# Attention scores issued two key tiles at a time, in a kernel whose plan gets new matmul times

## The chip, the core and the metric

The kernel runs on one core of a Trainium2 chip. The metric is device time in microseconds (us), the median of several executions. The kernel before took 481.65 us (480.47 to 483.04) when the prediction was made.

The engines are named as the profile names them: PE is TensorE (matmuls), PEld its weight loads, DVE is VectorE, ACT is ScalarE, POOL is GpSimd, SP is SyncE, which here only issues DMAs.

## The reference, cut to what matters

```python
batch, n_heads, seq, head_dim = (8, 12, 448, 64)
q_n, k_n = rmsnorm(q, g_q), rmsnorm(k, g_k)          # over head_dim
attn = softmax(matmul(q_n, k_n.T) / sqrt(64))
x = matmul(attn, v)                                  # -> (3584 tokens, 768)
h = x @ w_in                                         # 768 -> 2048
g = h * clip(h + 3, 0, 6) / 6
out = g @ w_out                                      # 2048 -> 768
```

The kernel works on 48 head pairs (8 batches of 6 pairs). One head has only 64 rows to contract, so the scores of the two heads of a pair use the upper and the lower half of the matmul array at once (in the trace of the kernel before, the two matmuls start 0.003 to 0.004 us apart). All other matmuls contract 112 or 128 rows.

## The kernel before

The kernel is not emitted in the order in which it is written. Every piece of work is recorded as a step with an engine, an estimated duration, a due time and its dependencies. A small list scheduler then replays these on modelled engines and emits the steps in the order of their modelled start. This fixes the instruction order of every engine when the program is built. The durations are only a model: on the chip nothing but the order is left of them.

```python
def order(self):                      # of class Plan, cut
    while len(done) < len(self.steps):
        # the engine that can start something first, by the model
        s = min((s for s in open_[e] if ready[id(s)] <= at), key=lambda s: (s.due, s.n))
        s.start = at
        free[e] = at + s.dur
        ...
    return sorted(done, key=lambda s: (s.start, s.n))
```

A step whose inputs are not ready in the model is passed over for one that is, whatever their due times.

PSUM holds two score buffers S, one buffer X and one R for the value products, and two buffers M shared by the MLP's matmuls. Per pair, four key tiles of 112 columns are scored and exponentiated:

```python
START, FIRST, SECOND, SLOT = 9.0, 4.1, 5.4, 7.9     # modelled length of a pair: 1st batch, 2nd, later
S_r = Ring(tiles("S", 2, [128, 2, 512], FP32, psum))
...
for t in range(T):                                   # T = 4
    ps, swar, s_use = S_r.take()
    def score(t=t, ps=ps):
        for a in range(2):
            rows = slice(a * 64, a * 64 + 64)
            nc.tensor.matmul(out=ps[:, a, 0:S], lhsT=kp[rows, t * PT:t * PT + 128],
                             rhs=kq[rows, 1, :], start=True, stop=True)
    s = add("PE", 0.25, at + step * t / T, score, *ks, *swar)
    x = add("ACT", 0.85, at + step * t / T + 0.2, ...EXP..., s, *war)
```

The work that feeds a pair ("preparation") runs on other engines: POOL squares q and k (sq), DVE sums (ssq), ACT makes rs, POOL scales (qks), SP issues a DMA transpose (kq<-qks), DVE makes kp.

## Time and profile before

| | before |
|---|---|
| time, median | 481.65 us |
| PE busy of 48 us, 160 to 208 and 208 to 256 us | 47.92 and 48.00 |
| first scores of pairs 3, 10 and 15 | 35.6, 95.0 and 130.9 us |
| twelve pairs, 24 to 36 | 103.4 us |

The first fence is from the page's groups; the columns after the first bar are busy time in all (us) and the mean of one (ns), then idle time of the engine just before them, with what ended most of it.

```profile
L336 PE MATMUL S<-kq,kp 64*128 64x448 bf16 x384 | 71.2, 384 | 11.1 <-ACT e L340 6.4
L336 PEld LDWEIGHTS <-kp 64*128 64x128 bf16 x384 | 18.2, 94 | 51.7 <-issue 41.9
```

The weight loads of the scores come after 41.9 us in which the weight loader waits for nothing that the profile shows. The next one is the table of stretches of the kernel before (start and end in us, length, then busy time of each engine):

```profile
core 0: us, PE busy (x) PEld busy (x) DVE busy (x) ACT busy (x) POOL busy (x), PEclk, DMA share, GB/s
64.00:112.00 48.00, 40.56 (x399) 22.02 (x395) 31.62 (x53) 33.89 (x60) 38.76 (x34) 0.96 0.76 159
112.00:160.00 48.00, 44.64 (x363) 22.32 (x364) 35.07 (x51) 30.22 (x57) 41.61 (x35) 1.00 0.86 197
208.00:256.00 48.00, 48.00 (x408) 24.41 (x407) 26.19 (x47) 29.09 (x47) 22.61 (x20) 1.00 0.62 148
```

From about 120 us PE is the bound; earlier it is not. A piece of PE's timeline (start, length, what) shows what a score costs:

```profile
208.79 0.36 PE L336 MATMUL S<-kq,kp 64*128 64x448 bf16 x2
209.08 0.43 PE L351 MATMUL X<-va,e 112*128 112x65 bf16 x8
209.45 0.36 PE L336 MATMUL S<-kq,kp 64*128 64x448 bf16 x2
209.74 0.43 PE L351 MATMUL X<-va,e 112*128 112x65 bf16 x8
210.01 0.42 PE L351 MATMUL R<-va,e 112*128 112x65 bf16 x8
```

Lengths overlap, so read the starts. Eight value matmuls take 210.01 - 209.74 = 0.27 us before more of their kind, but 209.45 - 209.08 = 0.37 before scores. The two matmuls of a lone key tile keep the array from 209.45 to 209.74, 0.29 us.

### The profile page before, as it was taken

The numbers are of one execution on the slowest core, as the hardware profiler recorded it, in microseconds if no ns is written. First come the engines' busy times: TensorE is split into PE (matmuls) and PEld (weight loads), VectorE is DVE, ScalarE is ACT, GpSimd is POOL, SyncE is SP. The second block draws the span as 40 slices with busy tenths as digits, with TensorE's granted clock in tenths as the row PEclk, the third lists the DMA queues.
The fourth block names the chain that finished last, engine by engine and source line by source line (L and its number), as shares of the span: only waits on it lengthen the run. The fifth ranks groups of instructions, "written<-read, shape, count | busy, mean of one in ns | idle before, by whom it ended". The sixth has DMA issues, their size and how long they took to land.

```text
span 480.8 us, 9258 instructions
## 1 busy us (share of the span) xinstructions
PE 436.2 (91%) x3658; PEld 237.9 (49%) x3658; DVE 246.6 (51%) x429; ACT 253.3 (53%) x421; POOL 220.9 (46%) x218
## 2 busy tenths in 40 slices
PE   0667698968999999999999999999999999999996
PEld 0334454534444555555445565554545555644463
DVE  2636457565877775454566445544444343433421
ACT  3445454885567565656676466655655555322200
POOL 7834866998789853655354634652231000000000
PEclk9985699998999999999999999999999999999999
DMA  7999984999787845766458567562413312211122
GB/s 190 245 245 240 251 183 111 187 194 210 194 231 135 204 102 132 169 169 160 117 132 154 134 148 174 120 172 55 99 29 73 78 49 51 59 34 33 34 64 67
DMA packets 103531, 65.26 MB, mean 136 GB/s; under 512 B 62400, under 2 KB 100032, under 8 KB 103488
## 3 DMA queue, kind: packets, MB, share of 16 engines
q1 hardware_dynamic: 98048, 58.38, 51.5%
q0 software_dynamic: 5440, 6.29, 7.4%
q8 instruction: 28, 0.46, 0.4%
q14 instruction: 15, 0.12, 0.1%
HBM read 45.61 MB, written 11.01 MB: 118 GB/s over the span
## 4 chain that ended last, share of the span: by engine, by line
PE 71%; POOL 10%; issue 8%; DMA 6%; DVE 2%; ACT 2%; POOLq 0%; ACTq 0%
PE M L472 30%; PE M L447 25%; PE S L336 8%; PE X L351 6%; POOL qks L280 4%; DMA w_in_sb<-in_moe_w_in_dram 4%; POOL sq L259 3%; PE R L351 2%; DMA kq<-qks 2%; POOL va L288 1%; DVE gT L455 1%; ACT t L453 1%; ACT e L340 1%; DVE kp L314 1%; POOL sq L251 0%
## 5 line engine op out<-in xcount | busy, mean ns | idle before, releaser
L340 ACT ACTIVATE e<-S 112x896 bf16<-112x896 f32 x192 | 171.4, 915 | 100.6 <-PE S L336 99.3
L447 PE MATMUL M<-xT,w_in_sb 128*128 128x384 bf16 (+1 forms) x768 | 170.5, 354 | 4.4 <-DVE y L480 1.9
L472 PE MATMUL M<-w_out_sb,gT 128*128 128x384 bf16 x896 | 161.6, 326 | 0.7 <-DVE gT L455 0.3
L280 POOL TENSOR_TENSOR qks<-qk,rs 112x512 bf16<-112x512 f32 x94 | 97.6, 1057 | 94.1 <-DMA kq<-qks 60.2
L455 DVE SCALAR_TENSOR_TENSOR gT<-t,M 128x384 bf16<-128x384 f32 (+1 forms) x128 | 79.2, 619 | 82.6 <-ACT t L453 82.3
L453 ACT ACTIVATE t<-M 128x384 f32<-128x384 f32 (+1 forms) x128 | 69.5, 543 | 81.8 <-PE M L447 78.6
L472 PEld LDWEIGHTS <-gT 128*128 128x128 bf16 x896 | 81.3, 98 | 60.1 <-issue 12.6
L447 PEld LDWEIGHTS <-w_in_sb 128*128 128x128 bf16 x768 | 66.8, 97 | 70.0 <-issue 21.1
L259 POOL TENSOR_TENSOR sq<-qk 112x1024 f32<-112x1024 f32 x41 | 78.5, 1919 | 20.1 <-DMA qk<-in_q_dram 13.8
L351 PEld LDWEIGHTS <-e 112*128 112x128 bf16 x1536 | 71.3, 102 | 31.0 <-issue 10.5
L336 PE MATMUL S<-kq,kp 64*128 64x448 bf16 x384 | 71.2, 384 | 11.1 <-ACT e L340 6.4
L480 DVE COPY y<-M 128x384 f32<-128x384 f32 x56 | 31.2, 557 | 70.0 <-PE M L472 70.0
L351 PE MATMUL X<-va,e 112*128 112x65 bf16 x1152 | 61.9, 201 | 1.9 <-ACT e L340 1.5
L262 DVE TENSOR_REDUCE ssq<-sq 112x16 f32<-112x1024 f32 x48 | 58.0, 1212 | 10.5 <-POOL sq L259 10.3
L288 POOL CAST va<-vf 112x512 bf16<-112x512 f32 x48 | 30.2, 630 | 31.7 <-PE R L351 18.1
L336 PEld LDWEIGHTS <-kp 64*128 64x128 bf16 x384 | 18.2, 94 | 51.7 <-issue 41.9
L314 DVE TENSOR_SCALAR kp<-kq,gp 128x448 bf16<-128x448 bf16 x41 | 24.5, 598 | 13.5 <-PE S L336 9.9
L377 DVE TENSOR_TENSOR xn<-X,rd 128x384 bf16<-128x384 f32 x48 | 26.8, 558 | 1.6
L300 PE MATMUL M<-ident,qks 112*128 112x112 bf16 x56 | 6.9, 284 | 21.5 <-DVE qks L280 14.7
L376 DVE RECIPROCAL rd<-X 128x6 f32<-128x6 f32 x48 | 9.3, 194 | 29.1 <-PE X L351 29.0
L351 PE MATMUL R<-va,e 112*128 112x65 bf16 x384 | 21.7, 201 | 0.0
L269 ACT ACTIVATE rs<-ssq 112x16 f32<-112x16 f32 x48 | 10.4, 216 | 12.7 <-POOL qks L280 6.7
(27 smaller groups left out, 69.3 us busy)
## 6 DMA issues: line engine op xcount, KB each, us to landing
qk<-in_k_dram SPq DMA_DIRECT2D x48, 224.0 KB, 3.6
qk<-in_q_dram SPq DMA_DIRECT2D x48, 224.0 KB, 3.9
vf<-in_v_dram SPq DMA_DIRECT2D x48, 224.0 KB, 3.8
w_in_sb<-in_moe_w_in_dram POOLq DMA_DIRECT2D x4, 768.0 KB, 22.1
w_out_sb<-in_moe_w_out_dram POOLq DMA_DIRECT2D x8, 384.0 KB, 28.5
out_dram<-y SPq DMA_DIRECT2D x8, 336.0 KB, 3.2
out_dram<-y SPq DMA_DIRECT2D x8, 288.0 KB, 2.7
out_dram<-y SPq DMA_DIRECT2D x8, 240.0 KB, 2.8
```

Source lines behind the costliest of these rows:

```text
L259: parts.append(add("POOL", 1.95, at - 12, lambda: nc.gpsimd.tensor_tensor(out=sq[0:PT], in0=qk[0:PT], in1=qk[0:PT], op=MULT), *ld, *war))
L262: red = add("DVE", 1.2, at - 8, lambda: nc.vector.tensor_reduce(out=ssq[0:PT], in_=sq[0:PT].rearrange("p i h (t d) -> p (i h t) d", d=D), ...
L280: nc.vector if e == "DVE" else nc.gpsimd).tensor_tensor(
L288: vc = add("POOL", 0.7, at - 3, lambda: nc.gpsimd.tensor_copy(out=va[0:PT, :, :, 0:D], in_=vf[0:PT].rearrange("p h (t d) -> p h t d", d=D) ...
L336: nc.tensor.matmul(out=ps[:, a, 0:S], lhsT=kp[rows, t * PT:t * PT + 128], rhs=kq[rows, 1, :], start=True, stop=True)
L340: x = add("ACT", 0.85, at + step * t / T + 0.2, lambda t=t, ps=ps: nc.scalar.activation(out=e[0:PT, t], in_=ps[0:PT, :, 0:S], func=EXP), s ...
L351: nc.tensor.matmul(out=dst[:, a * E1:(a + 1) * E1], lhsT=e[0:PT, t, a, c0:c0 + 128], rhs=va[0:PT, a, t, :], start=(first and a == 0 and t ...
L447: nc.tensor.matmul(out=m[:, 0:n], lhsT=w_in_sb[:, kt, f * 128:(f + 1) * 128], rhs=X[:, kt, :], start=(kt == 0), stop=(kt == NKT - 1))
L453: r = add("ACT", 0.08 + n / 1200, due + span, lambda: nc.scalar.activation(out=t[:, 0:n], in_=m[:, 0:n], func=RELU, bias=0.5, scale=1.0 / ...
L455: g = add("DVE", 0.12 + n / 960, due + span, lambda: nc.vector.scalar_tensor_tensor(out=G[:, f, :], in0=t[:, 0:n], scalar=1.0, in1=m[:, 0: ...
L472: nc.tensor.matmul(out=m[:, 0:HALF], lhsT=G[:, f, i * 128:(i + 1) * 128], rhs=w_out_sb[:, f, cols], start=(f == 0), stop=(f == NFT - 1))
L480: c = add("DVE", 0.55, due + span, lambda: nc.vector.tensor_copy(out=y[:, cols], in_=m[:, 0:HALF]), *parts, *(ywar if n == 0 else []))
```

## The change

From the second batch on, two key tiles are scored in one step, so that the array is switched to half-rows and back half as often. Such a cluster takes both score buffers, so it waits until both have been exponentiated. In the same edit the model's times for scores, exps and value products, and the slot of a pair, are set to what the trace shows.

```diff
-    START, FIRST, SECOND, SLOT = 9.0, 4.1, 5.4, 7.9
+    START, FIRST, SECOND, SLOT = 9.0, 4.1, 5.4, 8.3
 ...
-        for t in range(T):
-            ps, swar, s_use = S_r.take()
-            def score(t=t, ps=ps):
-                ... two matmuls, heads a = 0, 1 ...
-            s = add("PE", 0.25, at + step * t / T, score, *ks, *swar)
-            x = add("ACT", 0.85, ...)
+        size = 1 if P < NJ else 2
+        for t0 in range(0, T, size):
+            taken = [S_r.take() for _ in range(size)]
+            def score(t0=t0, taken=taken):
+                for i, (ps, _, _) in enumerate(taken):
+                    ... two matmuls, heads a = 0, 1 ...
+            s = add("PE", 0.2 + 0.196 * size, at + step * t0 / T, score, *ks, *(d for x in taken for d in x[1]))
+            for i, (ps, _, s_use) in enumerate(taken):
+                x = add("ACT", 0.93, ...)
 ...
-            av.append(add("PE", 0.31, ...values...        # also for `rest`
+            av.append(add("PE", 0.27, ...values...
 ...
-    mlp(B - 1, B - 2, end, end + 36.0, 2)                 # also in the line after it
+    mlp(B - 1, B - 2, end, end + 36.5, 2)
```

More of the change, by code (lines that the diff above doesn't have):

```diff
@@ L329, in attend @@
         exps = []
-        for t in range(T):
-            ps, swar, s_use = S_r.take()
-            def score(t=t, ps=ps):
-                for a in range(2):
-                    rows = slice(a * 64, a * 64 + 64)
-                    nc.tensor.matmul(out=ps[:, a, 0:S], lhsT=kp[rows, t * PT:t * PT + 128],
-                                     rhs=kq[rows, 1, :], start=True, stop=True)
-            s = add("PE", 0.25, at + step * t / T, score, *ks, *swar)
-            x = add("ACT", 0.85, at + step * t / T + 0.2, lambda t=t, ps=ps: nc.scalar.activation(
-                out=e[0:PT, t], in_=ps[0:PT, :, 0:S], func=EXP), s, *war)
-            s_use.append(x)
-            exps.append(x)
+        size = 1 if P < NJ else 2
[3 more added lines that the diff above has]
+                for i, (ps, _, _) in enumerate(taken):
+                    for a in range(2):
+                        rows, c0 = slice(a * 64, a * 64 + 64), (t0 + i) * PT
+                        nc.tensor.matmul(out=ps[:, a, 0:S], lhsT=kp[rows, c0:c0 + 128],
+                                         rhs=kq[rows, 1, :], start=True, stop=True)
+            s = add("PE", 0.2 + 0.196 * size, at + step * t0 / T, score, *ks, *(d for x in taken for d in x[1]))
+            for i, (ps, _, s_use) in enumerate(taken):
+                x = add("ACT", 0.93, at + step * (t0 + i) / T + 0.2, lambda t=t0 + i, ps=ps: nc.scalar.activation(
+                    out=e[0:PT, t], in_=ps[0:PT, :, 0:S], func=EXP), s, *war)
+                s_use.append(x)
+                exps.append(x)
             kq_use.append(s)
@@ L357, in attend @@
         for s in range(NS):
-            av.append(add("PE", 0.31, at + 0.15 * step * s, lambda s=s: values(
+            av.append(add("PE", 0.27, at + 0.15 * step * s, lambda s=s: values(
                 X[:, s * 130:(s + 1) * 130], s * 128, s == 0), *exps, vc, *war))
@@ L364, in attend @@
         i = P % 3
-        rest = add("PE", 0.31, at + 0.45 * step, lambda: values(
+        rest = add("PE", 0.27, at + 0.45 * step, lambda: values(
             Rt[:, i * 130:(i + 1) * 130], S - 128, i == 0), *exps, vc, *war)
@@ L549 @@
     end = begin[NP]
-    mlp(B - 1, B - 2, end, end + 36.0, 2)
-    mlp(None, B - 1, end + 36.0, end + 57.0, 0)
+    mlp(B - 1, B - 2, end, end + 36.5, 2)
+    mlp(None, B - 1, end + 36.5, end + 57.0, 0)
     with tc.manual_schedule():
```

## The prediction

> **What bounds the kernel now.** TensorE. In the table of stretches it is busy 47.9 to 48.0 of 48 us in each stretch from 160 to 400 us; ScalarE has 27 to 29 there, VectorE 19 to 28, GpSimd under 28. The chain of waits gives PE 71% of the span. Before about 120 us it is otherwise: PE idles until the first scores (16.5 us), then is starved behind loads, GpSimd (10.0 of 10 us in 80 to 90) and transposes. So from about 120 us on a microsecond of PE work removed is a microsecond of time; before that, nearly nothing.
>
> **What a score costs.** From starts of matmuls in PE's timeline: the two matmuls of one key tile (64 rows each) start 3 ns apart, and the next matmul of another kind 0.295 us after the first. Scores start 0.094 us later than the kind before them would start its next (eight value matmuls take 0.356 us before scores, 0.262 otherwise). Two key tiles in a row take 0.485 us, the second only 0.19. So two lone tiles cost 0.78 us, a cluster of two 0.58: 0.20 us saved. The Trainium skill, "TensorEngine Tiling (Array Packing)", Key Properties, says that changing the tiling mode drains the engine; the trace agrees, with these two gaps.
>
> **What changes in the order.** Comparing the built orders: as many matmuls, loads and activations as before. From the third batch on there are 126 runs of scores before (111 of one tile, 13 of two, 2 of three), 72 after, all of two; in the second batch 16 against 12. 58 fewer at 0.20 us: 11.5 us of PE time; my sum over those spacings goes from 413.4 to 401.9 us. Up to head pair 14 (115 us now) the sums are nearly equal, so it falls where PE is the bound. A pair's slot there goes from 8.6 to 8.3 us, which the new SLOT also says. The tail after the last scores (66 us) stays.
>
> **What it costs.** A cluster needs both score buffers, so it waits for two exps (1.72 us), and ScalarE idles some 0.4 us (scores, hops) before the next. From pair 14 on at least 2.6 us of PE work, mostly over 3.2, stand between clusters, so this should stay hidden. In the burst of pairs 8 to 13 (85 to 110 us), where ScalarE is 85 to 94% busy, only 0.4 to 0.9 us stand between them: PE will wait for exps there, up to 0.4 us a cluster; GpSimd's 4.6 us per pair covers most. I allow 1 us, and 2 us either way for other reordering of the static queues before 125 us (waits of 1.3 and 2.1 us there now).
>
> **Predicted:** 481.65 - 11.5 + 1 = 471.1 us, range 467.5 to 476. Faster by over 2% (under 472.0): 0.58; within 2%: 0.40; slower: 0.02.
>
> **What would show it.** PE's scores in clusters of four matmuls; PEld's idle before scores from 42 us to about 25; twelve pairs in 99.5 us instead of 103.4; PE full from 130 us on; the first score of pair 14 within 2 us of 115.
>
> **What would make it wrong.** A front end that moves by over 3 us; PE waits for exps inside the full stretch; relu evictions behind two exps in a row, so that both M buffers are held; the saved PE time exposing GpSimd (41.6 of 48 us in 112 to 160).

## More of the kernel before

After a pair, DVE normalizes X into xn, and SP transposes it (xT<-xn); the last 64 rows of three pairs go together as xr (xT<-xr). The MLP of a batch can start only when all its xT are there. POOL also issues the loads of the weights:

```python
for c in range(8):
    W_out[c] = add("POOL", 0.9, 36 + 3.5 * c, lambda c=c: load_w_out(c), xfer=2.7)
```

## The result, and the profile after

The changed kernel took 489.91 us (488.99 to 490.32, four runs), the kernel before 482.16 (four runs, three of them those above). The ratio is 1.0162 (95% interval 1.0129 to 1.0195): 1.6% slower, where 2.2% faster was predicted. A ratio here is the mean time of one kernel's runs over that of the other's of the same rounds, so not quite the ratio of the medians quoted.

What the change was meant to do, it did. The same two groups on the changed kernel's own lines:

```profile
L338 PE MATMUL S<-kq,kp 64*128 64x448 bf16 x384 | 61.6, 391 | 6.8 <-ACT e L343 5.7
L338 PEld LDWEIGHTS <-kp 64*128 64x128 bf16 x384 | 12.9, 96 | 26.1 <-issue 21.0
```

PE's timeline shows a cluster in the full stretch:

```profile
221.33 0.55 PE L338 MATMUL S<-kq,kp 64*128 64x448 bf16 x4
221.82 0.69 PE L354 MATMUL X<-va,e 112*128 112x65 bf16 x16
222.35 0.42 PE L354 MATMUL R<-va,e 112*128 112x65 bf16 x8
```

Two tiles take 221.82 - 221.33 = 0.49 us, where two lone ones took 0.29 each and had a late start twice. The unexplained wait of the weight loader is halved. The table of stretches of the changed kernel:

```profile
64.00:112.00 48.00, 38.47 (x333) 20.92 (x330) 29.40 (x49) 27.83 (x55) 38.67 (x34) 0.86 0.64 143
112.00:160.00 48.00, 41.02 (x350) 20.86 (x349) 31.43 (x47) 29.15 (x55) 38.78 (x32) 0.87 0.76 176
208.00:256.00 48.00, 47.87 (x421) 26.00 (x418) 28.13 (x49) 29.53 (x51) 25.80 (x25) 1.00 0.63 156
```

PE has more instructions in the full stretch, but fewer between 64 and 160 us, where it is also granted a lower clock (0.86 and 0.87). The first score of a pair, read from PE's timelines, dates the loss (differences are taken before rounding):

| first scores of pair | 3 | 6 | 10 | 11 | 13 | 15 | 24 | 36 | 47 | end |
|---|---|---|---|---|---|---|---|---|---|---|
| before, us | 35.6 | 59.2 | 95.0 | 98.7 | 107.4 | 130.9 | 208.8 | 312.2 | 407.5 | 480.8 |
| changed, us | 42.4 | 64.7 | 102.0 | 111.2 | 120.2 | 145.7 | 221.3 | 322.9 | 415.1 | 488.2 |
| later by | 6.8 | 5.5 | 7.0 | 12.5 | 12.8 | 14.8 | 12.5 | 10.6 | 7.6 | 7.4 |

So 6.8 us are lost at pair 3, in the first batch, where there is no cluster at all. About as much again is lost between pairs 10 and 15. From there to the end the changed kernel gains 7.4 us back.

**The first loss.** Here are POOL's timelines, first before, then changed; at the end of a line stands the idle time before it.

```profile
31.21 0.72 POOL L215 DMA_DIRECT2D w_out_sb<-in_moe_w_out_dram  x1 [5.57 <-DMA w_in_sb<-in_moe_w_in_dram]
31.95 1.06 POOL L280 TENSOR_TENSOR qks<-qk,rs 112x512 bf16<-112x512 f32 x1
...
33.51 1.04 POOL L280 TENSOR_TENSOR qks<-qk,rs 112x512 bf16<-112x512 f32 x1
37.65 0.77 POOL L215 DMA_DIRECT2D w_out_sb<-in_moe_w_out_dram  x1 [3.10 <-DMA w_in_sb<-in_moe_w_in_dram]
```

```profile
31.23 0.71 POOL L215 DMA_DIRECT2D w_out_sb<-in_moe_w_out_dram  x1 [5.61 <-DMA w_in_sb<-in_moe_w_in_dram]
37.57 0.71 POOL L215 DMA_DIRECT2D w_out_sb<-in_moe_w_out_dram  x1 [5.62 <-DMA w_in_sb<-in_moe_w_in_dram]
38.28 0.62 POOL L288 CAST va<-vf 112x512 bf16<-112x512 f32 x1
38.86 2.04 POOL L280 TENSOR_TENSOR qks<-qk,rs 112x512 bf16<-112x512 f32 x2
```

Each of these two issues of a w_out load stands in POOL's queue until an earlier w_in load has landed; in the trace it waits for the very semaphore that it will use itself. The model gives such an issue 0.9 us. In the new order the last of them stands ahead of the scaling for pair 3, which had been ahead of it, and pair 3's scaling moves from 31.95 to 38.86 us. PE stands for it:

```profile
29.16 0.50 PE L393 MATMUL M<-ident,xn 128*128 128x128 bf16 x3
39.97 0.56 PE L300 MATMUL M<-ident,qks 112*128 112x112 bf16 x4 [10.30 <-POOL qks L280]
```

**The second loss.** From pair 10 on PE waits for exps and for X in the changed kernel, and at the end of the burst (pairs 8 to 13) for the last transpose of batch 1. The first fence is from PE's timeline, the second from a table of stretches (columns as above, PEclk is the granted share of the clock):

```profile
121.51 1.47 PE L450 MATMUL M<-xT,w_in_sb 128*128 128x512 bf16 x3
127.25 4.00 PE L450 MATMUL M<-xT,w_in_sb 128*128 128x512 bf16 x9 [4.27 <-DMA xT<-xr]
...
134.65 2.10 PE L450 MATMUL M<-xT,w_in_sb 128*128 128x512 bf16 x9
```

```profile
118.00:121.40 3.40, 2.19 (x36) 1.35 (x36) 3.27 (x8) 2.21 (x5) 2.86 (x4) 1.00 1.02 259
121.40:131.60 10.20, 5.93 (x23) 1.84 (x20) 3.63 (x5) 3.36 (x9) 9.61 (x9) 0.50 1.04 195
```

The wait of 4.27 us is followed by nine matmuls in 4.00 us; the same nine take 2.10 us a little later, so another 1.9 us are lost there, at half clock. The Trainium skill, "TensorE: Matmul & The Clock Gate", Part 1 (What's actually happening), says that the array's clock falls back to half after an idle window of some 3.4 us. This trace does not fit that: the clock was at half before the long wait began. It fell at 121.4 us, the three matmuls before the wait are as slow as those after it (1.47 us for three), and in the 3.4 us before it fell PE was busy for 2.19 us and had no gap over 0.60 us.

Half clock is a large part of this loss. The table adds up PE's matmuls from the first score of pair 6 to that of pair 15, with the stretches that the trace records at half clock. The other runs in it are told of below.

| pair 6 to pair 15, us | length | PE idle | PE busy at half clock |
|---|---|---|---|
| before | 71.7 | 10.5 | 5.0 |
| changed | 81.0 | 16.2 | 16.1 |
| clusters alone | 79.7 | 14.9 | 16.8 |
| times alone | 71.6 | 9.9 | 5.3 |
| SP alone held | 72.0 | 9.0 | 13.4 |
| late clusters | 71.6 | 8.9 | 9.3 |
| both repairs | 75.7 | 9.9 | 21.1 |

(The traces of "SP alone held" and "both repairs" lack 23 and 24 of 3658 matmul records, so their sums are rough.) The changed kernel idles 5.7 us more and works 11.1 us more at half clock. As nine matmuls take 4.00 us there instead of 2.10, an estimate is that nearly half of these 11.1 us, some 5 us, are lost. No run changes the clock alone, so what makes it fall is not shown.

Why that burst is slower is not plain from the trace: clusters that wait for two exps, new times in the model, or an order on some other engine are all possible. The experiments are about this.

### The profile page after: what moved, and what is told of

Same layout as the page of the kernel before. It is cut to its first block, busy times and chain, and to the rows that moved or that the text cites. A ratio compares the mean times of both kernels' runs of the same rounds, so it can differ in the third digit from the quotient of the medians.

```text
span 488.2 us, 9283 instructions
## 1 busy us (share of the span) xinstructions
PE 430.0 (88%) x3658; PEld 238.7 (49%) x3658; DVE 248.0 (51%) x429; ACT 250.7 (51%) x421; POOL 220.9 (45%) x218
## 4 chain that ended last, share of the span: by engine, by line
PE 65%; DVE 5%; POOL 3%; issue 2%; ACT 2%; DMA 2%; ACTq 0%; POOLq 0%; DVEq 0%
PE M L475 30%; PE M L450 22%; PE S L338 6%; PE X L354 6%; DVE gT L458 3%; POOL qks L280 2%; PE R L354 2%; ACT t L456 1%; DVE ssq L262 1%; DMA xT<-xr 1%; POOL sq L259 1%; DVE kp L314 1%; DMA kq<-qks 1%; ACT e L343 1%; POOL va L288 0%
## 5 line engine op out<-in xcount | busy, mean ns | idle before, releaser
L343 ACT ACTIVATE e<-S 112x896 bf16<-112x896 f32 x192 | 168.0, 913 | 92.1 <-PE S L338 90.9
L475 PE MATMUL M<-w_out_sb,gT 128*128 128x384 bf16 x896 | 158.8, 326 | 2.0 <-DVE gT L458 1.5
L475 PEld LDWEIGHTS <-gT 128*128 128x128 bf16 x896 | 83.2, 98 | 64.8 <-issue 14.1
L450 PEld LDWEIGHTS <-w_in_sb 128*128 128x128 bf16 x768 | 69.6, 98 | 80.9 <-issue 30.1
L354 PEld LDWEIGHTS <-e 112*128 112x128 bf16 x1536 | 72.3, 103 | 42.1 <-ACT e L343 9.7
L354 PE MATMUL X<-va,e 112*128 112x65 bf16 x1152 | 64.2, 201 | 10.5 <-ACT e L343 7.5
L338 PE MATMUL S<-kq,kp 64*128 64x448 bf16 x384 | 61.6, 391 | 6.8 <-ACT e L343 5.7
L314 DVE TENSOR_SCALAR kp<-kq,gp 128x448 bf16<-128x448 bf16 x41 | 26.7, 652 | 16.7 <-DMA kq<-qks 8.7
L300 PE MATMUL M<-ident,qks 112*128 112x112 bf16 x56 | 7.2, 289 | 26.7 <-DVE qks L280 14.8
L338 PEld LDWEIGHTS <-kp 64*128 64x128 bf16 x384 | 12.9, 96 | 26.1 <-issue 21.0
```

What stands on the lines that cost most here:

```text
L314: ks = add("DVE", 0.25, at - 1, lambda: nc.vector.tensor_scalar_mul(kp[:, 0:S], kq[:, 0], gp[:, 0:1]), tr, g_make, one_make, *kwar)
L338: nc.tensor.matmul(out=ps[:, a, 0:S], lhsT=kp[rows, c0:c0 + 128], rhs=kq[rows, 1, :], start=True, stop=True)
L343: x = add("ACT", 0.93, at + step * (t0 + i) / T + 0.2, lambda t=t0 + i, ps=ps: nc.scalar.activation(out=e[0:PT, t], in_=ps[0:PT, :, 0:S], ...
L354: nc.tensor.matmul(out=dst[:, a * E1:(a + 1) * E1], lhsT=e[0:PT, t, a, c0:c0 + 128], rhs=va[0:PT, a, t, :], start=(first and a == 0 and t ...
L450: nc.tensor.matmul(out=m[:, 0:n], lhsT=w_in_sb[:, kt, f * 128:(f + 1) * 128], rhs=X[:, kt, :], start=(kt == 0), stop=(kt == NKT - 1))
L475: nc.tensor.matmul(out=m[:, 0:HALF], lhsT=G[:, f, i * 128:(i + 1) * 128], rhs=w_out_sb[:, f, cols], start=(f == 0), stop=(f == NFT - 1))
```

## The experiments

Theory 1 was: the loss is one POOL load moved by the new model times, plus a burst slowed by the clusters; the gain of the full stretch is there. The rival: the new times did it all, and clusters are innocent. All kernels gave right results. In this section a ratio compares with the kernel before of the same rounds, but times of different rounds are also subtracted (the kernel before took 482.32 to 483.24 us in them). Every table row below that names a pair is the first score of that pair in the profiled run, a single execution.

### Clusters alone, times alone, late clusters, the load put back

Clusters with the old times (a_clusters_only):

```diff
-s = add("PE", 0.2 + 0.196 * size, ...     exps 0.93, values 0.27, SLOT 8.3, end + 36.5
+s = add("PE", 0.25 * size, ...            exps 0.85, values 0.31, SLOT 7.9, end + 36.0
```

> Clusters of two from the second batch on, but the old model times (score 0.25 us a tile, exp 0.85, values 0.31, slot 7.9). Its order is before's up to the first scores of pair 7, and its w_out loads stand as in before. Theory 1 (the loss of the change is two things: one w_out load moved ahead of pair 3's scaling by the new model times, about 6 us, and a slower burst of pairs 8 to 14 with clusters, about 9 us): pair 6 starts its scores at 59 us as before, pair 15 about 8 to 10 us later than before's 130.9, the full stretch gains about 8 us; total 481 to 485 us. Rival (the new model times did all the harm, clusters are innocent): pair 15 within 3 us of 130.9, total 472 to 475 us.

New times without clusters (b_times_only):

```diff
-        size = 1 if P < NJ else 2
+        size = 1
```

> The new model times without any clusters. Its GpSimd order has the w_out load ahead of pair 3's scaling as the changed kernel has. Theory 1: pair 3 starts its scores at 42 us instead of 35.6, pairs 8 to 13 at before's pace, pair 15 about 6 us late, no gain after; total 487 to 490 us. Rival (new times did all the harm): pair 15 at 146 us, some 15 us late; total 496 to 499 us.

Clusters only from pair 14 on, old times (c_late_clusters):

```diff
-        size = 1 if P < NJ else 2
+        size = 1 if P < 14 else 2          # and the old times, as above
```

> Clusters only from pair 14 on, old model times; the orders of all engines are before's up to pair 14. Both theories of the loss: front end as before (pair 15 at 131 us within 1.5), then the gain that the full stretch gives: 10.7 us of PE work less than before by the count of score runs (413.4 to 402.7 us), less up to 3 us of new waits; total 472 to 475 us. If clusters cost something inside the full stretch that the count misses, total above 477.

The changed kernel with one dependency more (e_load_after_scale):

```diff
         qk_use += parts + sc
+        if P == 3:
+            W_out[6].deps += sc            # this load is issued after pair 3's scaling
```

> The changed kernel with one dependency more in its plan: the seventh w_out load is issued after pair 3's scaling. ScalarE's order is then exactly the changed kernel's. Theory 1: pair 3's scores start at about 35.6 us instead of 42.4, and most of that carries to the end: 6 us less than the changed kernel, 483 to 486 us. If the early loss is absorbed by the burst's own waits (loads, GpSimd), the total stays within 2 us of 490.

| | pair 3 | pair 10 | pair 15 | end | time, median | ratio to before (95%) |
|---|---|---|---|---|---|---|
| before | 35.6 | 95.0 | 130.9 | 480.8 | 482.32 | |
| clusters alone | 34.7 | 95.9 | 138.2 | 482.2 | 483.85 | 1.0042 (1.0015 to 1.0068) |
| times alone | 42.1 | 96.6 | 135.7 | 489.8 | 493.16 | 1.0224 (1.0195 to 1.0253) |
| late clusters | 33.9 | 94.3 | 129.3 | 474.3 | 474.72 | 0.9842 (0.9809 to 0.9876) |
| load put back | 34.7 | 95.1 | 138.7 | 481.7 | 483.86 | 1.0019 (0.9967 to 1.0070) |

Four things follow. The early loss belongs to the new model times: it comes with them and without clusters, and one dependency takes it away; that is worth 489.91 - 483.86 = 6.0 us. The burst's loss belongs to the clusters: from pair 6 to pair 15 it takes 79.7 us with them under the old times, and 71.6 under the new times without them (71.7 before). Clusters where the burst is over are a clear gain, 7.6 us. The times-alone run was slower than theory 1 had it (487 to 490) and faster than the rival had it (496 to 499): besides the load, its stretch from pair 15 to 47 takes 280.5 us against 276.6 before. New times alone make the order of the full stretch worse.

### Is it VectorE's kp, or the waiting for two exps?

In the changed kernel's DVE queue, kp of pair 12 (which waits for a DMA transpose) stands ahead of the normalization of pair 9's X; in the kernel before it stands behind it. Theory 1a was that this blocks X. The rival, 1b, was that clusters are slow because they wait for two exps.

```diff
             qks_use.append(tr)
+            ks.deps.append(XN[P - 3])      # kp of pair P after X of pair P-3 is normalized
```

With this on top of the repaired load (f_both_fixes):

> The changed kernel with the load dependency of the earlier run and one more: VectorE makes kp of pair P (which waits for a DMA transpose) only after it has normalized pair P-3's X. Clusters, model times and slot stay. Theory 1a (the burst is slow because VectorE's in-order queue stands at kp of pair 12 and 13 while the X normalization that frees the single X buffer, and the sums that feed GpSimd, stand behind it): PE waits of 3.8, 2.3 and 2.5 us at pairs 11 to 14 go, pair 15 starts at 130 to 133 us instead of 138.7; total 475 to 478 us. Rival 1b (the burst is slow because each cluster waits for two exps): pair 15 stays within 2 us of 138.7, total 482 to 485 us.

With this on top of clusters alone (f2_clusters_kp):

> Clusters with the old model times and the same VectorE order (kp of pair P after X of pair P-3 is normalized), against the clusters-only run that had pair 15 at 138.2 us and 483.9 us in total. Theory 1a: pair 15 at 129 to 133 us, total 475 to 478 us. Rival 1b: pair 15 at 137 to 139, total 482 to 485 us.

They took 484.03 and 485.90 us, with pair 15 at 138.4 and 138.7. **Theory 1a fell.** Yet something moved: in the second of them pair 13 came at 110.7 us instead of 113.5, and the time was lost again in a wait of 6.5 us for the last transposes of batch 1 (6.9 in an expectation below; the trace has 6.46). So freeing one engine's queue only handed the wait on, and the waiting for two exps was not all of it either.

In the same round the late clusters were tried with the new times too, for pairs from 14 on (d_late_new_times):

```diff
-... 0.25 * size ... 0.85 ... 0.31
+... 0.25 if P < 14 else 0.592 ... 0.85 if P < 14 else 0.93 ... 0.31 if P < 14 else 0.27
```

> Clusters from pair 14 on as in the run of 474.7 us, with the new model times too, but for steps of pairs from 14 on alone; front orders are before's. If the new times make the order of the full stretch better (fewer late evictions: that run had a wait of 2.7 us at 197 us and 6.7 us of excess from 150 us on), 471 to 473 us; if they do nothing, 473 to 476 us.

It took 474.55 us (0.9825, 0.9791 to 0.9858), no different from late clusters with the old times. For pairs from 14 on, the new times neither help nor harm.

### Holding the other queues fixed

Theory 1c took the place of 1a: with clusters the plan lets preparation run further ahead, so that in the queues of the helping engines loads and kq transposes stand before the last work of batch 1. To test it, the order of an engine was taken from the kernel before as a table, and the scheduler was allowed to choose only the next step of that table.

```diff
+FORCE = {"SP": [0, 1, 3, 4, 2, ...], ...}   # steps of that engine in before's order
 ...
+    if e in queue:
+        l = [s for s in l if s is queue[e][-1]]
```

With clusters and the old times, SP, DVE and POOL held to before's orders (m_three_orders):

> Clusters from the second batch on, old model times (the clusters-only run of 483.9 us), but the queues of SyncE, VectorE and GpSimd keep before's orders literally; only the orders of PE and ScalarE are planned anew. The theory that VectorE's kp alone did it has fallen (the burst to pair 13 came back by 2.8 us, the wait of the w_in matmuls of batch 1 for the last transposed xr grew to 6.9 us). Theory 1c (clusters let preparation run a pair further ahead in the plan, so in all three queues loads, kq transposes and kp stand ahead of the last work of batch 1, which arrives late): pair 15 at 129 to 133 us instead of 138.2, the wait of w_in for xr under 2 us, total 474 to 478 us. Rival 1b (waiting for two exps slows the burst, whatever the queues): pair 15 at 136 us or later, total 481 to 485 us.

The same with the new times (m_new_three):

> The changed kernel whole, clusters and new model times and slot, but the queues of SyncE, VectorE and GpSimd keep before's orders. Under theory 1c the new times harm only through those queues (the w_out load ahead of pair 3's scaling is one case): pair 3 at 35 us, pair 15 at 129 to 133, total 473 to 478 us. If the order of PE under the new times is itself bad, total over 480.

With clusters and the old times, SP alone held (n_sp_order):

> The clusters-only kernel with before's order on SyncE's queue alone, VectorE and GpSimd planned anew. If the late xr transpose (SyncE issued it 5.7 us after it was made, behind a kq transpose and loads) is the larger part, pair 15 comes to 131 to 134 us, total 476 to 480. If VectorE or GpSimd hold the chain as well, pair 15 stays above 135 and the total above 480.

The reverse (r_reverse): no clusters, but SP, DVE and POOL in the orders of the clusters-alone kernel.

> The other way round: no clusters, old model times, but SyncE, VectorE and GpSimd follow the clusters-only kernel's orders literally. Theory 1c: the loss comes without any cluster, PE idle between 80 and 150 us grows from before's 13 us to 18 or more, total 488 to 493 us. Rival 1b: PE idle there as before's within 2 us, total 481 to 485 us.

| | pair 3 | pair 10 | pair 13 | pair 15 | end | time, median | ratio to before (95%) |
|---|---|---|---|---|---|---|---|
| clusters alone, again | 34.7 | 95.9 | 113.5 | 138.2 | 482.2 | 483.85 | 1.0042 |
| three queues held | 34.9 | 97.0 | 110.2 | 130.8 | 473.9 | 478.59 | 0.9909 (0.9861 to 0.9957) |
| same, new times | 34.4 | 97.9 | 114.0 | 134.0 | 478.6 | 480.78 | 0.9967 (0.9916 to 1.0017) |
| SP alone held | 35.1 | 97.3 | 111.4 | 131.0 | 474.8 | 475.36 | 0.9860 (0.9819 to 0.9900) |
| reverse | 34.2 | 96.6 | 108.9 | 121.8 | 494.5 | 498.92 | 1.0333 (1.0285 to 1.0382) |

Holding SP's queue alone brings pair 15 from 138.2 to 131.0 us, and the time from 483.85 to 475.36: 8.5 us, with the clusters of the burst still in place. That is the larger part of the second loss. From pair 6 to pair 15 PE idles 5.9 us less and works 3.4 us less at half clock (the table above). The traces show where the idle goes. First clusters alone, from SP's, DVE's and PE's timelines:

```profile
111.60 0.56 DVE L420 TENSOR_TENSOR xr<-R,rd 64x384 bf16<-64x384 f32 x1
...
110.25 1.59 SPq L311 DMA_TRANSPOSE kq<-qks  x1
111.90 0.57 SPq L232 DMA_DIRECT2D qk<-in_k_dram  x1
112.52 0.45 SPq L232 DMA_DIRECT2D qk<-in_q_dram  x1
113.07 1.18 SPq L403 DMA_TRANSPOSE xT<-xn  x1
114.35 1.20 SPq L428 DMA_TRANSPOSE xT<-xr  x1
...
114.80 0.81 PE L450 MATMUL M<-xT,w_in_sb 128*128 128x512 bf16 x3
119.23 2.29 PE L450 MATMUL M<-xT,w_in_sb 128*128 128x512 bf16 x5 [3.63 <-DMA xT<-xr]
```

Then the run with SP's queue held:

```profile
109.84 0.56 DVE L444 TENSOR_TENSOR xr<-R,rd 64x384 bf16<-64x384 f32 x1
...
109.61 1.18 SPq L427 DMA_TRANSPOSE xT<-xn  x1
110.88 1.21 SPq L452 DMA_TRANSPOSE xT<-xr  x1
...
113.62 0.61 PE L474 MATMUL M<-xT,w_in_sb 128*128 128x512 bf16 x1
114.40 2.32 PE L474 MATMUL M<-xT,w_in_sb 128*128 128x512 bf16 x10 [0.16 <-issue]
```

With its own order, SP has a kq transpose and two loads for later pairs ahead of the last xn and xr of batch 1. It takes 1.59 us for that transpose and 0.57 and 0.45 for the loads before it reaches them. The xr that was made at 111.60 + 0.56 = 112.16 us is issued at 114.35, 2.2 us later; with the queue held it is issued 0.5 us after it was made. It is also made 1.8 us earlier, so the delay had been going round through the other engines as well. The wait of 3.63 us for it is gone. (The 5.7 us of the expectation belong to the run f2_clusters_kp, where xr is made at 109.33 us and issued at 115.00.)

The reverse run agrees in direction, 3.3% slower without any cluster in it (498.92 us, where 488 to 493 was expected), but it is not clean. The scheduler, given those queues, also moved PE's work: pair 15 was placed before the MLP of batch 1, and the full stretch became slower too (299.4 us from pair 15 to 47, against 276.6). Its size says nothing about the burst.

The same-with-new-times run missed its expectation (473 to 478): X's matmuls wait 7.4 us for exps between 60 and 150 us. The order of PE and ScalarE under the new times seems to cost a few microseconds in the burst too. The run with three queues held also missed, by 0.6 us; its profiled execution took 475.68 us, the fastest of its four, so its pair times look better than its median.

### The two repairs together, and the full stretch

The changed kernel with SP's queue held and the load put back (p_after_sp_fix):

> The changed kernel whole (clusters, new times, slot 8.3) with two repairs only: SyncE's queue in before's order, and the seventh w_out load after pair 3's scaling. If these two places in two queues are the loss of the changed kernel, as the clusters-only kernel with SyncE's order (475.4 us) and the run with the load moved (6 us gained) say, pair 3 starts at 35 us, pair 15 at 130 to 134 us, and the total is 474 to 478 us, some 13 us under the changed kernel. If the new times do more harm than that one load, the total is over 480.

Late clusters with SP's queue held to the end (q_late_sp):

> Clusters from pair 14 on, old times (474.7 us in an earlier run, with 6.3 us of PE idle between 150 and 415 us where before has 1.4), with SyncE's queue in before's order to the end. If the new idle of the full stretch comes from SyncE's order as the burst's did, that idle falls to under 3 us and the total to 470 to 472 us; if it comes from PE's and ScalarE's own order, idle and total stay within 1.5 us.

The first took 476.95 us (0.9896, 0.9861 to 0.9932), pair 3 at 35.7 and pair 15 at 134.9. So one load and the order of SP's queue account for 489.91 - 476.95 = 13.0 us of the changed kernel's time: 6.0 for the load and 6.9 more for SP's order. Pair 15 missed its range (130 to 134 us) in the profiled execution, which was the slowest of the four (479.54 us). The second took 474.57 us, no different from 474.72. SP's order does not make the idle that is left in the full stretch. (Its trace lacks 23 records of w_in matmuls, so idle can't be summed from it over the full stretch; the time decides. The traces of all runs with held queues, of the two kp runs and of d_late_new_times lack 23 or 24. All scores are there, but their idle times are rough.)

What that idle is, the waits of PE between 150 and 415 us say (in all, times, longest). First before, then late clusters:

```profile
PE S L336 <- ACT e L340: 0.6, 1, 0.6
```

```profile
PE M L450 <- DVE y L483: 2.6, 1, 2.6
PE M L450 <- DVE gT L458: 1.4, 4, 0.5
PE M L475 <- DVE gT L458: 0.8, 2, 0.7
```

PE hardly waits for exps; it waits for an M buffer that DVE has not emptied. The longest one, in DVE's timeline of that run:

```profile
198.11 1.22 DVE L262 TENSOR_REDUCE ssq<-sq 112x16 f32<-112x1024 f32 x1 [3.60 <-POOL sq L259]
199.25 0.55 DVE L483 COPY y<-M 128x384 f32<-128x384 f32 x1
```

DVE stands 3.60 us at a sum of preparation that POOL has not squared yet, and the copy that would free the M buffer stands behind it. It looks like the same fault once more: a step of preparation, ready in the model, is ahead of one that PE needs. No run tested this.

## Why the prediction was wrong

**Right.** PE bounds the kernel from about 120 us. A lone tile is dear and a second one cheap: the cluster takes 0.49 us, and the weight loader's idle before scores fell from 41.9 to 21.0 us (about 25 predicted). The Trainium skill, "TensorEngine Tiling (Array Packing)", Key Properties, which the prediction named for the drain at a change of mode, agrees with the trace: eight value matmuls take 0.37 us before scores and 0.27 otherwise. The gain is also there in time: late clusters alone give 7.6 us.

**The step that failed** is this one: "I allow 1 us, and 2 us either way for other reordering of the static queues before 125 us". Pair 15, which should have come about as early as before, came 14.8 us late. The order of PE had been compared with care, matmul by matmul, and its sums up to pair 14 were nearly equal. From this the prediction took it that the front end would stay. But the front end was not bound by PE: its time is in the queues of POOL, SP and DVE, and of these the prediction compares only how many loads and activations there are. It had named "a front end that moves by over 3 us" as what would make it wrong, and this is what happened: with the load put back and SP's order held, 13.0 us come back. The move that cost 6.0 us, one load ahead of one scaling, stood in POOL's order before any run. What it would cost was in the trace as well: the issue of that kind just before it stands 5.57 us.

**Also wrong, "the first score of pair 14 within 2 us of 115".** It came at 136.9 us. Part of this is that the new plan puts more of the MLP before pair 14; pair 15 is the fairer mark.

**Mis-sized: the gain of the full stretch.** Twelve pairs were to take 99.5 us and take 101.5 (before 103.4). Of the 11.5 us of PE time, which were to fall where PE is the bound, 7.4 came from pair 15 to the end. PE was not quite full there (46.68 to 48.00 of 48 us in the stretches from 160 to 400, 47.92 to 48.00 before). The prediction's list of risks had M buffers held by late evictions, and these are what PE waits for between 150 and 415 us (2.9 us in the changed kernel, 4.8 in the late-cluster run, none listed before). The cause that it gave, evictions behind two exps, was not tested; the longest wait of the late-cluster run shows another, preparation in the way.

**Right, once SP's queue is held: the burst's own cost.** That PE would wait there for exps was right. With SP's queue held, pair 15 comes at 131.0, and with no clusters in the burst at 129.3, but 1.2 us of this difference are there at pair 3, before any cluster. From pair 6 to pair 15 it is 72.0 against 71.6 us, inside the 1 us that was allowed; these are single executions.

**Still open.** Which single entry of SP's queue starts the delay was not isolated; the whole order was held. The remaining difference between 476.95 us and the 474.7 of late clusters was not split by a run; its profiled execution has PE busy at half clock for 21.1 us from pair 6 to pair 15 (9.3 with late clusters). What makes the clock fall, and whether it falls alike in every execution, is open too.

The best kernels found have clusters from pair 14 on. They take 474.72 us with the old times and 474.55 with the new ones, 1.6 to 1.8% under the kernel before; the two can't be told apart.

## What to carry to other kernels

Where a plan fixes the order of every engine, a change of its durations is a change of the program: compare the order of each engine's queue before and after, above all of the engines that bound the stretch, not only that of the engine the change is about. A DMA issue, or a step that waits for a DMA and so can stand for microseconds, must not be placed, by a model that does not know this, ahead of what the bound engine will soon need. And apply a good local change first where its engine is the bound: the same clusters gain 7.6 us when they start at pair 14, and lose it all when they also cover the burst before, unless SP's order is held as it was (475.36 us).

## What the Trainium skill lacked or had wrong

- "TensorEngine Tiling (Array Packing)", Key Properties, says that a change of mode drains the array, but gives no size. Here a run of scores in half-row mode costs 0.09 to 0.10 us before it (eight value matmuls 0.37 us instead of 0.27), and a second tile in the same run adds only 0.19 to 0.20 us to the 0.29 of the first; so one run fewer saves about 0.20 us.
- "TensorE: Matmul & The Clock Gate", in the table at its head, calls the queues of ScalarE, VectorE and GpSimd strict FIFO, which these traces bear out for two of them (DVE stands 3.60 us at one sum with a ready copy behind it; on POOL the scaling for pair 3 waits behind a load issue until 38.86 us). It does not list SyncE. Here the order of SyncE's DMA issues alone was worth 8.5 us, at 1.2 to 1.6 us of its queue for a DMA transpose and about 0.5 us for a load.
- I found on no page that the issue of a load from GpSimd can hold up the computing that follows it in that queue. Here two w_out issues stood 5.6 us each, on a semaphore that an earlier load had still to signal.
- "TensorE: Matmul & The Clock Gate", Part 1 (What's actually happening), gives an idle window of some 3.4 us as what drops the clock to half. Here it fell at 121.4 us after 3.4 us in which PE was busy for 2.19 us, with no gap over 0.60 us.
